# A spectral filter and MLP block, forward and backward: the fourth row block of h kept on chip, the other h loads put into spent slots, and all five engine orders laid out anew

## The chip, the core and the metric

The kernel runs on one core of a Trainium2 chip. The metric is the device time of one execution in microseconds (us); less is better. The times of the kernel before are 394.0, 394.21 and 395.75 us, median 394.21.

## The reference

An adaLN block on x of 2048 rows by 512, bf16, and its gradient. Six modulation rows come from a vector c; a spectral filter stands in the place of attention, an MLP with a squared ReLU behind it:

```python
mod = (silu(c) @ w_mod).reshape(c.shape[0], 6, 1, -1)
sa, ca, ga, sb, cb, gb = ...
h = layernorm(x) * (1 + ca) + sa
x = x + ga * irfft2(rfft2(h) * (w_r + 1j * w_i))
n = layernorm(x) * (1 + cb) + sb
h = relu(n @ w1 + b1) ** 2          # 2048 x 1792
x = x + gb * (h @ w2 + b2)
```

The outputs are the block's result and the gradients with respect to x, w_r, w_i, w1, b1, w2, b2, c and w_mod, ten in all. The gradient of w2 is h transposed times the scaled incoming gradient, the gradient of w1 is the normalized rows transposed times the gradient at h.

## The kernel before

Rows are worked on in 16 tiles of 128 (t), grouped in four blocks of 512 rows (b, NB = 4). The MLP's width of 1792 is cut into 14 chunks of 128 (fc, NFC = 14). The two-dimensional Fourier transforms are matmuls with constant matrices.

The stages, in the order in which the work is written:

- The start: filler matmuls on a tile of ones (L751, 30 of them), the modulation rows, the layernorm statistics (L819, L820), the constants TA of the transform (L119 to L130, on VectorE, ScalarE and TensorE), sacol (L757), the product L787 of sacol with a part of w_mod and its doubling gb2x (L789), w2 transposed and scaled by it (L796, L799), the first transform.
- back_products (L887): w2 transposed times the incoming gradient, written to gaT, a part of the large tile gall.
- The forward spectral pass.
- For each row block b: stage_g, stage_m and stage_t make the second layernorm and its transposes; stage_h (L1051) makes h and its gradient, seven pairs of chunks, each in a tile "h" of a ring of seven buffers, and writes each pair to h_dram (L1074); ghn_part (L1045) transposes the gradient at h from SBUF to SBUF into ghn, other rows of gall, 28 DMAs in all (gab<-gab in the trace); stage_gn and stage_o make the back product of the MLP and the block's result (L1096).
- The second spectral pass, backward (L1360 to L1425): its element-wise steps run on VectorE (L444 to L447, in cmul) and read Z and Xb from DRAM (L1373, L1377).
- grad_w1 (L1338 to L1349): 16 units that use ghn and h_sb, the normalized rows loaded back from DRAM at L1234. The first eight units, with fb 0 and 1, use the first seven chunks of ghn.
- The last row pairs (row_pair, L1504 on): VectorE and ScalarE finish the gradient of x, with gs, gh1 and q1 as ring tiles; colsums1 (L1499) sums gh1 and q1 on TensorE.
- grad_w2 (L1433 to L1443): 14 chunks of 16 matmuls of 128 by 512 in g_sb times hn, and g_sb is the gradient scaled by one modulation row (L1463). hn is a chunk of h with rows on the partitions, which the DMA transposes as it loads it from h_dram (load_hn, L1252 to L1257): 16 tiles of 128 by 128, 512 KB. The first two chunks lie in a pool hnp, the next two in a pool of the second pass, and the rest in a ring of six in the pool endp. After chunk fc, loads are issued up to the larger of fc + 4 and the smaller of 2 fc + 6 and 10.
- The modulation gradients (GMod: wmc loads L481, gm_junk on VectorE L500, gwm stores L502), and the tail.

Nearly all transfers are issued from SyncE (SP), whose queue is in order: an issue that waits holds back all issues behind it. The order of every engine's instructions is fixed by the table ORDER (L505 to L600): for each of the five engines it lists the instructions' numbers, by program position, in the order in which they are to run, and set_order (L603) ties each to the one before it.

```python
def set_order(tc):
    ...
    for name, runs in ORDER.items():
        todo = mine[ENGINES[name]]
        ...
        for before, after in zip(seq, seq[1:]):
            tc.add_manual_dep(after, before.name, edge, reason="order")
```

Of the kernel before, what the change touches and what calls it, by code (L numbers as in the profile page):

```python
# [18 lines left out]
D = 512  # L19
# [5 lines left out]
NB = 4  # L25
# [444 lines left out]
class GMod:  # L470
# [12 lines left out]
    def emit(self, jc, q, row, pool, ppool, nbuf=2, last=False):  # L483
# [1134 lines left out]
```

## Time and profile before

| what | value |
|---|---|
| times of the runs | 394.0, 394.21, 395.75 us |
| median | 394.21 us |
| the profiled execution's own time, from its first to its last instruction | 398.0 us |
| TensorE (PE) busy | 382.1 us, 96% |
| VectorE (DVE) busy | 334.8 us, 84% |
| ScalarE (ACT) busy | 303.2 us, 76% |
| HBM traffic | 181 GB/s over the span |
| mean granted TensorE clock | 0.990 |

The profile is one execution, and the trace gives 398.0 us for it, 3.8 us above the median of the timed runs. In the page each engine has a row of 40 slices, a digit for the busy share in tenths, and PEclk is the clock that TensorE was granted. The view of the waits has rows "engine output line <- what it waited for: us in total, times, longest". The chain of waits and the timelines give the start in us, then the duration in us. "SPq" is SyncE's queue: the time of such a row is that of the issue, and "to landing" is the time from issue until the data are there. L is the line in the kernel.

### The profile page before, as it was taken

Reading aid. Unit: us, or ns where it says so; the run is one execution under the profiler, and the core shown is the slowest. Engines: PE = TensorE matmul, PEld = TensorE weight load, DVE = VectorE, ACT = ScalarE, POOL = GpSimd, SP = SyncE. Lnnn points to the kernel's source line nnn. Section 1 sums busy time; section 2 is a strip of 40 time slices with the busy share of each in tenths; the row PEclk is TensorE's granted clock in tenths of the full one; section 3 lists DMA queues with packets and bytes.
Section 4 is the critical chain, followed back from the end, with each engine's and each line's share of the span. In section 5 each row is a group of like instructions: output and inputs, shape, how many; then the busy total and the mean of one; then the engine's idle time right before and its main releaser. Section 6 shows DMA issues by size and latency. Waiting matters only on the chain.

```text
span 398.0 us, 8415 instructions
## 1 busy us (share of the span) xinstructions
PE 382.1 (96%) x3042; PEld 202.4 (51%) x3042; DVE 334.8 (84%) x822; ACT 303.2 (76%) x605; POOL 33.3 (8%) x114
## 2 busy tenths in 40 slices
PE   8999999999999999999999999999999999999495
PEld 3555677544444444444444435457666664444244
DVE  8899959949986699969997999957999989998430
ACT  4787899899896499759976999277665589998441
POOL 9151001000000000000000000012300000002100
PEclk9999999999999999999999999999999999999979
DMA  8999799874589999578928696999979998999995
GB/s 258 362 222 293 230 209 252 209 280 63 195 228 197 256 259 253 128 191 183 257 81 210 167 245 180 270 245 371 296 221 262 215 325 173 221 208 243 249 259 189
DMA packets 133957, 91.06 MB, mean 229 GB/s; under 512 B 86842, under 2 KB 119868, under 8 KB 133660
## 3 DMA queue, kind: packets, MB, share of 16 engines
q1 hardware_dynamic: 132904, 88.09, 87.1%
q0 software_dynamic: 832, 2.36, 1.8%
q8 instruction: 24, 0.39, 0.4%
q14 instruction: 17, 0.14, 0.1%
q10 hardware_dynamic: 180, 0.07, 0.1%
HBM read 38.70 MB, written 33.19 MB: 181 GB/s over the span
## 4 chain that ended last, share of the span: by engine, by line
PE 74%; ACT 12%; DMA 5%; DVE 4%; POOL 2%; issue 1%; SPq 0%; ACTq 0%; POOLq 0%; DVEq 0%
PE og_1s L1096 12%; PE og_0s L1096 11%; PE mm_0s L1441 6%; PE mm_1s L1441 6%; PE mm_0s L1342 5%; PE mm_1s L1342 5%; PE mm_1s L1064 4%; PE mm_0s L1064 4%; PE pst L1064 3%; DMA hn_1s<-h_dram 3%; PE mm_0s L892 2%; DMA Xb<-xs_dram 2%; ACT AE L359 2%; PE mm_1s L892 2%; ACT gab L896 2%; ACT gab L1073 1%
## 5 line engine op out<-in xcount | busy, mean ns | idle before, releaser
L1342 PEld LDWEIGHTS <-h_sb 128*64 128x64 bf16 (+1 forms) x464 | 28.7, 109 | 15.9 <-issue 0.9
L1073 ACT ACTIVATE gab<-gab 128x512 bf16<-128x512 bf16 x56 | 35.0, 648 | 0.5 <-DVE gab L1071 0.5
L1096 PEld LDWEIGHTS <-gab 128*128 128x128 bf16 x224 | 21.5, 98 | 27.0 <-ACT gab L1073 1.9
L1064 PEld LDWEIGHTS <-w 128*128 128x128 bf16 x224 | 21.2, 98 | 25.7 <-issue 1.7
L1342 PE MATMUL mm_0s<-gab,h_sb 128*64 128x384 bf16 (+2 forms) x288 | 32.7, 345 | 0.0
L892 PEld LDWEIGHTS <-w2T 128*128 128x128 bf16 (+1 forms) x280 | 22.9, 102 | 18.5 <-issue 3.9
L1096 PE MATMUL og_0s<-w1T,gab 128*128 128x512 bf16 x112 | 27.4, 379 | 0.2 <-ACT G_0s L1109 0.2
L1096 PE MATMUL og_1s<-w1T,gab 128*128 128x512 bf16 x112 | 27.6, 379 | 0.0
L1441 PE MATMUL mm_0s<-g_sb,hn_1s 128*128 128x512 bf16 x64 | 16.8, 423 | 6.0 <-DMA hn_1s<-h_dram 6.0
L1342 PE MATMUL mm_1s<-gab,h_sb 128*64 128x512 bf16 (+2 forms) x176 | 22.4, 370 | 0.0
L1064 PE MATMUL mm_1s<-h2T,w 128*128 128x512 bf16 x84 | 21.9, 379 | 0.0
L1064 PE MATMUL mm_0s<-h2T,w 128*128 128x512 bf16 x80 | 21.2, 379 | 0.0
L359 ACT ACTIVATE AE<-psB 128x1024 bf16<-128x1024 f32 x16 | 17.2, 1078 | 0.7 <-PE psB L355 0.6
L896 ACT CAST gab<-mm_1s 128x512 bf16<-128x512 f32 x24 | 14.8, 615 | 2.3 <-PE mm_1s L892 2.2
L892 PE MATMUL mm_0s<-gT_0s,w2T 128*64 128x512 bf16 (+1 forms) x76 | 16.1, 380 | 0.2 <-DVE gab L894 0.2
L892 PE MATMUL mm_1s<-gT_0s,w2T 128*128 128x512 bf16 (+1 forms) x72 | 15.6, 379 | 0.1
L1064 PE MATMUL pst<-h2T,w 128*128 128x512 bf16 x60 | 15.6, 379 | 0.0
L892 PE MATMUL mm_1s<-gT_1s,w2T 128*128 128x512 bf16 (+1 forms) x68 | 14.9, 379 | 0.3 <-ACT gab L896 0.2
L892 PE MATMUL mm_0s<-gT_1s,w2T 128*128 128x512 bf16 (+1 forms) x64 | 15.1, 379 | 0.0
L1441 PEld LDWEIGHTS <-hn_1s 128*128 128x128 bf16 x64 | 6.8, 107 | 15.3 <-DMA hn_1s<-h_dram 6.2
L321 POOL MEMSET AE<- 128x4 bf16 x4 | 0.4, 110 | 162.4 <-PE mm_1s L1064 162.4
L1441 PE MATMUL mm_1s<-g_sb,hn_0s 128*128 128x512 bf16 (+1 forms) x64 | 13.7, 352 | 0.0
(650 smaller groups left out, 1064.3 us busy)
## 6 DMA issues: line engine op xcount, KB each, us to landing
w<-in_B_w_dram SPq DMA_DIRECT2D x2, 1792.0 KB, 10.4
Xb<-xs_dram SPq DMA_DIRECT2D x4, 514.0 KB, 7.9
Z<-wz_dram SPq DMA_DIRECT2D x4, 514.0 KB, 7.5
x_sb<-in_A_x_dram SPq DMA_DIRECT2D x4, 512.0 KB, 6.2
n_dram<-x_sb SPq DMA_DIRECT2D x4, 512.0 KB, 6.2
h_dram<-h2r SPq DMA_DIRECT2D x8, 256.0 KB, 2.4
h_sb<-h_dram SPq DMA_DIRECT2D x4, 512.0 KB, 5.4
g_sb<-in_grad_out_dram SPq DMA_DIRECT2D x2, 1024.0 KB
```

Source lines behind the costliest of these rows:

```text
L321: nc.gpsimd.memset(ae[:, :, :, 256:257], 0.0)
L359: nc.scalar.activation(dst, ps.rearrange("p r b (e f) -> p (r b) f e", e=2), AF.Copy, scale=EF_S)
L892: nc.tensor.matmul(ps[m], lhsT=w2T[:, dc, fc * P + m.start:fc * P + m.stop], rhs=gT[b][:, :, dc, :], start=(dc == 0), stop=(dc == 3), **pos)
L896: nc.scalar.copy(out=gaT[b][:, fc, :], in_=ps)
L1064: nc.tensor.matmul(ps, lhsT=w1[:, dc, (fc + i) * P:(fc + i + 1) * P], rhs=h2T[b][:, :, dc, :], start=(dc == 0), stop=(dc == 3))
L1073: nc.scalar.activation(gh[:, i, :], gh[:, i, :], AF.Copy, accum_out=gb1[:, b, fc + i:fc + i + 1])
L1096: nc.tensor.matmul(ps, lhsT=lhs(fc), rhs=rhs[:, fc, :], start=(fc == 0), stop=(fc == NFC - 1))
L1342: nc.tensor.matmul(blocks(ps[m], fb), lhsT=h2_sb[:, t, dc * P + m.start:dc * P + m.stop], rhs=gh_rows(t, fb), start=(t == 0), stop=(t == N ...
L1441: nc.tensor.matmul(ps[:, 0:w], lhsT=hns[fc][:, t, :], rhs=g_sb[:, t, c:c + w], start=(t == 0), stop=(t == NT - 1))
```

## The change

Its parts:

- h_dram holds three row blocks instead of four. stage_h writes the chunks of blocks 0 to 2 as before; for block 3 nothing is written, and hpair keeps the seven tiles of the ring.
- Those seven tiles are transposed by the DMA from SBUF to SBUF into a new tile hr, among stage_gn of block 3 ("turns"). h_rows returns rows of hr for the last four row tiles and rows of hn for the others.
- load_hn loads 12 row tiles instead of 16, 384 KB instead of 512, into slots of gall which held ghn for the first eight units of grad_w1: eight slots, chunk fc and chunk fc + 8 share one. After chunk fc, loads are issued up to chunk fc + 9. Four loads instead of two are issued at each of the two places in the program ahead of grad_w2.
- The rings of gs, gh1, q1 and gw in the last stages lie in other spent rows of gall (Ring and place, over "spare") instead of the pool endp. The pools hnp and endp are gone; gall is released at the end.
- A pool "early" takes n2rows of the even blocks, h2r, h2T and r, and is released ahead of stage_gn of block 3.
- The table ORDER is laid out anew on all five engines.

```diff
-    h_dram = dram.tile([NFC, P, NT * P], BF16, name="h_dram")
+    h_dram = dram.tile([NFC, P, (NT - TB) * P], BF16, name="h_dram")
...
+    early = Slots(tc, name="early", bufs=1)
...
-                    n2b[b] = rows.tile([P, TB, D], BF16, name="n2rows")
+                    n2b[b] = (rows if b % 2 else early).tile([P, TB, D], BF16, name="n2rows", bufs=1)
...
-                nc.sync.dma_start(h_dram[fc:fc + 2, :, sl].rearrange("a p s -> p a s"), h2)
+                if b < NB - 1:
+                    nc.sync.dma_start(h_dram[fc:fc + 2, :, sl].rearrange("a p s -> p a s"), h2)
+                else:
+                    hpair[fc] = h2
...
-                merge(stage_gn(b, UT), [x for p in zip(again, parts + [lambda: None]) for x in p])
+                hrp = Slots(tc, name="hrp", bufs=1, side="right")
+                hr = hrp.tile([P, NFC, TB, P], BF16, name="hr")
+                turns = [lambda fc=fc: nc.sync.dma_start(hr[:, fc:fc + 2].rearrange("p a j c -> p (a j) c"), hpair[fc].rearrange("p a s -> p (a s)"), transpose=True)
+                         for fc in range(0, NFC, 2)]
+                merge(stage_gn(b, UT), [x for p in zip(again, parts + [lambda: None], turns + [lambda: None]) for x in p])
...
+    spare = [NFC * b + 6 for b in range(NB)] + [NFC * b + k for b in range(NB) for k in range(7, NFC)] + [NB * NFC, NB * NFC + 1]
+
+    def place(n):
+        a = next(a for a in spare if all(a + k in spare for k in range(n)))
+        for k in range(n):
+            spare.remove(a + k)
+        return gall[:, a:a + n, :]
+
+    class Ring:
+        def __init__(self, n, k):
+            self.tiles, self.k = [place(n) for _ in range(k)], 0
+
+        def tile(self):
+            self.k += 1
+            return self.tiles[(self.k - 1) % len(self.tiles)]
...
-            pool = hnp if fc < 2 else endp.get("hn", endp["gw"])
-            hns.append(pool.tile([P, NT, P], BF16, name="hn", bufs=2 if pool is not endp.get("hn") else 6))
+            a = NFC * (fc % 4) + 3 * (fc // 4 % 2)
+            hns.append(gall[:, a:a + 3, :].rearrange("p a (j c) -> p (a j) c", c=P))
             nc.sync.dma_start(hns[fc], h_dram[fc, :, :], transpose=True)
+
+    def h_rows(fc, t):
+        return hns[fc][:, t, :] if t < NT - TB else hr[:, fc, t - (NT - TB), :]
...
-                nc.tensor.matmul(ps[:, 0:w], lhsT=hns[fc][:, t, :], rhs=g_sb[:, t, c:c + w], start=(t == 0), stop=(t == NT - 1))
+                nc.tensor.matmul(ps[:, 0:w], lhsT=h_rows(fc, t), rhs=g_sb[:, t, c:c + w], start=(t == 0), stop=(t == NT - 1))
...
-        while len(hns) < min(NFC, max(fc + 4, min(2 * fc + 6, 10))):
+        while len(hns) < min(NFC, fc + 9):
             load_hn()
...
-                    endp["hn"] = endp["gm"] = Slots(tc, name="endp", bufs=2)
+                    endp["gs"], endp["gh1"], endp["q1"], endp["gw8"] = Ring(2, 6), Ring(2, 3), Ring(2, 3), Ring(1, 8)
...
     "PE": (
-        "0-7 30 8-13 31 14-16 52-59 17-22 32-47 23-26 64-67 27 60-63 28 76-83 29 68-75 89-93 237-240 84-88 99-103 241-242 245-246 "
+        "1 0 3 2 4 6 8 5 10 7 9 30 11-13 15 14 17 19 52 31 16 53-54 18 55 32-47 56-59 20-21 23 64-67 60-63 25 27 29 76-83 68-75 "
```

In the changed kernel the lines stand lower: the h write is L1084, ghn_part L1058, the hr transposes L1244, the h_sb loads L1251, load_hn L1288, grad_w1 L1376 to L1383, the scaling of g_sb L1497, grad_w2 L1475 and L1477; at the start the fillers are L758, sacol L764, gb2x L796, the statistics L826.

First place, SyncE at the end of the program, before. hn_0s to hn_3s are chunks of h, wmc the parts of w_mod for its gradient, out_6 the gradient of w2, gxl rows for the gradient of x.

```order
L481 DMA wmc_0s_5631<-in_w_mod_dram 128x4x512
L1443 DMA out_6_dram<-gw_1s_5350 128x512
L1257 DMA_TRANSPOSE hn_0s_5723<-h_dram_65 128x16x128
L1334 DMA gxl_1s_5519<-gx1_dram_62 128x1024
L1257 DMA_TRANSPOSE hn_1s_5774<-h_dram_65 128x16x128
L1443 DMA out_6_dram<-gw_2s_5374 128x512
L1257 DMA_TRANSPOSE hn_2s_5796<-h_dram_65 128x16x128
L481 DMA wmc_1s_5633<-in_w_mod_dram 128x4x512
L1257 DMA_TRANSPOSE hn_3s_5824<-h_dram_65 128x16x128
L1443 DMA out_6_dram<-gw_3s_5450 128x512
```

And now, where gab is gall and holds the chunks of h as well as the tiles of gw:

```order
L1477 DMA out_6_dram<-gab_145 128x512
L1436 DMA out_2_dram<-Xb_4067 32x4x257
L1477 DMA out_6_dram<-gab_145 128x512
L1433 DMA out_2_dram<-Xb_4067 32x2x1028
L1288 DMA_TRANSPOSE gab_145<-h_dram_65 128x12x128
L1368 DMA gxl_5344<-gx1_dram_62 128x1024
L1368 DMA gxl_1s_5502<-gx1_dram_62 128x1024
L481 DMA wmc_0s_5611<-in_w_mod_dram 128x4x512
L1477 DMA out_6_dram<-gab_145 128x512
L481 DMA wmc_1s_5613<-in_w_mod_dram 128x4x512
```

The row with h_dram is the last of the 14 loads. Before, four loads stand among the last stores and the wmc loads; now the last one stands ahead of both wmc loads, and the others stand further up.

Second place, SyncE around block 3's last stages, before. h_2s to h_6s are the pairs of h, gab<-gab the transposes of the gradient at h, LFb and Cdb constants of the second pass, h_sb the rows for grad_w1.

```order
L1074 DMA h_dram<-h_4s 128x2x512
L1228 DMA LFb_3510<-LF_dram 128x1024
L1228 DMA LFb_3509<-LF_dram 128x1024
L1049 DMA_TRANSPOSE gab<-gab 128x8x128
L1074 DMA h_dram<-h_6s 128x2x512
L1074 DMA h_dram<-h_5s 128x2x512
L1049 DMA_TRANSPOSE gab<-gab 128x8x128 x2
L1134 DMA gx_dram<-n2rows_1s 128x1024
L1234 DMA h_sb<-h_dram 128x2048 x2
```

And now:

```order
L1244 DMA_TRANSPOSE hr<-h_3s 128x8x128
L1244 DMA_TRANSPOSE hr<-h_0s 128x8x128
L1058 DMA_TRANSPOSE gab<-gab 128x8x128
L1244 DMA_TRANSPOSE hr<-h_2s 128x8x128
L1146 DMA gx_dram<-n2rows 128x1024
L1251 DMA h_sb<-h_dram 128x2048
L1244 DMA_TRANSPOSE hr<-h_6s 128x8x128
L1244 DMA_TRANSPOSE hr<-h_4s 128x8x128
L1058 DMA_TRANSPOSE gab<-gab 128x8x128
L1236 DMA Cdb<-Cd_dram 128x512
L1251 DMA h_sb<-h_dram 128x2048 x3
```

Where plain writes of h stood, transposes of h into hr stand, three ahead of the first h_sb load and two more ahead of the last three.

Third place, VectorE at the start, before. ta_v is what TA is made from, l_st and l_mv are the layernorm statistics of x, gen_v and lf the parts of other constants.

```order
L119 SCALAR_TENSOR_TENSOR ta_v<-kh,pidf,kh_off 128x128
L755 CAST ccolf<-sm_ps 128x4
L121 TENSOR_SCALAR ta_v<-ta_v 128x128
L757 TENSOR_TENSOR sacol<-sigcol,ccolf 128x4
L176 TENSOR_SCALAR gen_v_1s<-cf_dr,cf_f_1180 128x128
L764 CAST scf<-sacol 128x4
L176 TENSOR_SCALAR gen_v_1s<-cf_dr,cf_f_1180 128x128
L819 BN_STATS l_st_0s<-x_sb 128x6
L819 BN_STATS l_st_2s<-x_sb 128x6
```

And now, from the first statistic on; sacol follows 12 rows further down, behind the next aggregate and parts of lf:

```order
L826 BN_STATS l_st_2s<-x_sb 128x6
L224 TENSOR_SCALAR lf_ph<-lf_tf 128x1 x2
L227 TENSOR_SCALAR lf_ph<-lf_tf 128x1
L826 BN_STATS l_st_3s<-x_sb 128x6
L826 BN_STATS l_st_0s<-x_sb 128x6
L227 TENSOR_SCALAR lf_ph<-lf_tf 128x1
L827 BN_AGGR l_mv_1s<-l_st_3s 128x2
L231 TENSOR_SCALAR lf_mk<-lf_sm,lf_tf 128x16
L119 SCALAR_TENSOR_TENSOR ta_v<-kh,pidf,kh_off 128x128
```

Three statistics stand ahead of ta_v and of sacol, where they stood behind both.

More of the change, by code (lines that the diff above doesn't have):

```diff
@@ L963 @@
         ghn = [None] * NB
+        hpair = {}
         late, late_f1 = Delayed(4), Delayed(4)
@@ L1015, in one @@
                 t = TB * b + j
-                h2r = rows.tile([P, 2, D], BF16, name="h2r", bufs=1)
+                h2r = early.tile([P, 2, D], BF16, name="h2r")
                 nc.vector.tensor_tensor(h2r, n2b[b][:, j:j + 2, :], modb[:, CB1_B, None, :].broadcast_to([P, 2, D]), op=ALU.mult)
@@ L1021, in one @@
                     if j == 0:
-                        h2T[b] = rows.tile([P, TB, 4, P], BF16, name="h2T", bufs=1)
+                        h2T[b] = early.tile([P, TB, 4, P], BF16, name="h2T")
                     K["h2T"] = nc.sync.dma_start(h2T[b][:, j:j + 2].rearrange("p j c q -> p (j c) q"), h2r.rearrange("p j d -> p (j d)"),
@@ L1030, in one @@
                 if j == 0:
-                    h2T[b] = rows.tile([P, TB, 4, P], BF16, name="h2T", bufs=1)
+                    h2T[b] = early.tile([P, TB, 4, P], BF16, name="h2T")
                 pst = psR.tile([P, D], FP32, name="pst2").bitcast(BF16).rearrange("p (c i q) -> p c i q", c=4, i=2)
@@ L1056, in stage_h @@
             for fc in range(0, NFC, 2):
-                r = rows.tile([P, 2, SB], BF16, name="r")
+                r = early.tile([P, 2, SB], BF16, name="r", bufs=2)
                 for i in range(2):
@@ L1219 @@
             else:
+                early.release()
                 w1p.release()
@@ L1248 @@
     gm = GMod(tc, K, scf, gsc, wm_view, out9_view)
-    hnp = Slots(tc, name="hnp", bufs=1, side="right")
     hns, endp = [], {}
+    spare = [NFC * b + 6 for b in range(NB)] + [NFC * b + k for b in range(NB) for k in range(7, NFC)] + [NB * NFC, NB * NFC + 1]
[10 more added lines that the diff above has]
+            return self.tiles[(self.k - 1) % len(self.tiles)]
     def load_hn():
@@ L1422, in after_b @@
                     K["g_load"] = nc.sync.dma_start(endp["g_sb"][:, t:t + 8, :], g_view[:, t:t + 8, :]).ins
-                load_hn()
-                load_hn()
+                for _ in range(4):
+                    load_hn()
         spec_f23(tc, K, UT, AEs, None, lambda gi: gwa.tile([P, 2, 2, FP], BF16, name="G", bufs=2), ew_b, after_b)
@@ L1434, in grad_w2 @@
         if cols[0] == 0:
-            late_ = "gm" in endp
-            gwh[fc] = (endp["gm"] if late_ else gwp).tile([P, D], BF16, name="gw", bufs=8 if late_ else 2)
+            late_ = "gw8" in endp
+            gwh[fc] = endp["gw8"].tile()[:, 0, :] if late_ else gwp.tile([P, D], BF16, name="gw", bufs=2)
         gw = gwh[fc]
@@ L1452, in grad_b2 @@
         add_quadrants(ps, gwp, out_7[None, :])
-    for _ in range(2):
+    for _ in range(4):
         load_hn()
@@ L1484, in fill @@
                     gwa.release()
-                    gap.release()
-                    endp["hn"] = endp["gm"] = Slots(tc, name="endp", bufs=2)
+                    endp["gs"], endp["gh1"], endp["q1"], endp["gw8"] = Ring(2, 6), Ring(2, 3), Ring(2, 3), Ring(1, 8)
                     endp["q"] = Slots(tc, name="endq", bufs=2)
@@ L1505, in row_pair @@
             n1, gxl = rows3[t]
-            gh1, q1 = [(endp["gm"].tile([P, 2, D], BF16, name=x, bufs=3) if "gm" in endp and t >= 6 else fp.tile([P, 2, D], BF16, name=x, bufs=2)) for x in ("gh1", "q1")]
+            gh1, q1 = [(endp[x].tile() if "gs" in endp and t >= 6 else fp.tile([P, 2, D], BF16, name=x, bufs=2)) for x in ("gh1", "q1")]
             gn = fp.tile([P, 2, D], BF16, name="gn")
-            gs = (endp["gm"].tile([P, 2, D], BF16, name="gs", bufs=6) if "gm" in endp and t >= 6 else fp.tile([P, 2, D], BF16, name="gs", bufs=3))
+            gs = (endp["gs"].tile() if "gs" in endp and t >= 6 else fp.tile([P, 2, D], BF16, name="gs", bufs=3))
             rr = fp.tile([P, 2, 4], FP32, name="rr")
@@ L1576 @@
     lf2.release()
-    hnp.release()
     h2p.release()
+    hrp.release()
     cdp.release()
@@ L1582 @@
     endp["q"].release()
-    endp["gm"].release()
+    gap.release()
     set_order(tc)
```

171 rows, old and new, of the table ORDER are left out of this document.

## The prediction

> **What bounds the kernel now.** I read the page first, for which engine fills the span and where it does not.
>
> ```profile
> span 398.0 us, 8415 instructions
> PE 382.1 (96%) x3042; PEld 202.4 (51%) x3042; DVE 334.8 (84%) x822; ACT 303.2 (76%) x605; POOL 33.3 (8%) x114
> PE   8999999999999999999999999999999999999495
> PEclk9999999999999999999999999999999999999979
> ```
>
> TensorE is busy for 96% of the span. The clock row and the PE row dip together once, near the end; every other slice after the first is full. So there are two sorts of gain: less PE work, of which the change removes none, or the dip. The view of the waits, for PE, says how large the dip is:
>
> ```profile
> PE mm_0s L1441 <- DMA hn_1s<-h_dram: 6.0, 1, 6.0
> PE mm_0s L751 <- DVE ones_sq L83: 1.8, 1, 1.8
> PE psB L355 <- ACT AE L359: 0.8, 2, 0.7
> PE psW_1s L796 <- ACT gT_0s L811: 0.4, 1, 0.4
> ```
>
> One wait of 6.0 us, for a transposed load of h; the 1.8 us are ahead of filler matmuls at the start; the rest is under a microsecond each. The chain of waits gives the same place in time, and SyncE's timeline shows the queue that fed it (start, duration of the issue):
>
> ```profile
> 366.24 12.07 DMA hn_1s<-h_dram
> 378.36 5.97 PE mm_0s L1441 x16
> 384.33 3.45 PE mm_1s L1441 x16
> ```
>
> ```profile
> 361.15 4.37 SPq L1257 DMA_TRANSPOSE hn_0s<-h_dram  x1
> 366.24 5.22 SPq L1257 DMA_TRANSPOSE hn_1s<-h_dram  x1
> 372.41 7.57 SPq L1257 DMA_TRANSPOSE hn_2s<-h_dram  x1
> DMA to landing us min/median/max: 4.9/5.7/12.1
> ```
>
> The load of chunk hn_1 was issued at 366.24, and PE was ready for it at 378.36 − 6.0 = 372.4, so it had 6.2 us; its median landing is 5.7 us (last row, L1257's), but this one took 12.1. Then the first unit of 16 matmuls after the gap takes 5.97 us where the next takes 3.45: the slow clock of the dip costs a further 2.5 us. The stall is thus worth 6.0 + 2.5 = 8.5 us.
>
> The view of stages shows what the transfers and VectorE have left (us, PE busy, PEld, DVE, ACT, POOL, then PE clock, DMA share, GB/s):
>
> ```profile
> 235.00:262.00 27.00, 26.78 (x165) 12.30 (x163) 26.29 (x59) 16.81 (x37) 1.31 (x5) 1.00 0.90 236
> 262.00:300.00 38.00, 37.09 (x500) 25.93 (x500) 30.84 (x75) 25.80 (x42) 6.76 (x15) 1.00 0.94 292
> 300.00:345.00 45.00, 45.00 (x512) 25.41 (x509) 42.97 (x97) 34.80 (x72) 0.00 (x0) 1.00 0.96 241
> 345.00:372.00 27.00, 27.00 (x150) 12.41 (x149) 24.24 (x58) 24.48 (x49) 4.54 (x9) 1.00 1.08 223
> 372.00:384.00 12.00, 6.04 (x20) 2.24 (x19) 2.02 (x6) 4.14 (x8) 0.33 (x1) 0.72 1.15 247
> ```
>
> The DMA engines are full from 235 on, and past full from 345; PE's clock is 1.00 until 372. So the transfers are the second bound, and VectorE (43.0 of 45 us between 300 and 345) is the third.
>
> **The loads of h (the gain).** Each of the 14 loads shrinks from 16 to 12 rows, 512 to 384 KB, and goes into a slot that grad_w1 has finished with, up to nine chunks ahead. Chunk 13 has the slot of chunk 5, so its load can start when unit 5 is done, with units 6 to 12 still ahead of its own; in the order (the first place shown) it now stands ahead of both wmc loads and the last stores of gw, where before it came behind both. A unit is 3.45 us, so a lead of up to 7 × 3.45 = 24 us replaces 6.2, where even the worst landing was 12.1. Per microsecond of PE work the loads of the last third also ask for a quarter less. I take the whole stall as gone: −6.0 and −2.5. What is late next: the wmc loads stood in front of the last hn loads before and now follow them, but only the modulation gradient's tail needs them, beside about 24 us of PE units.
>
> **Block 3's h, on chip.** Seven writes of 256 KB go; seven DMA transposes of 256 KB SBUF to SBUF come. The near row is the kernel's own transposes of gab, the same shape (issue, then landing), against the landing of the h writes (L1074):
>
> ```profile
> L1049 SPq DMA_TRANSPOSE gab<-gab x28: 1231/1239/2031, 128.2 to 262.2; - x28
> DMA to landing us min/median/max: 3.1/3.1/5.4
> SPq L1049 <- DMA gab<-gab: 19.9, 17, 3.3
> DMA to landing us min/median/max: 2.2/2.9/8.7
> ```
>
> Low end 7 × 1.24 = 8.7 us of the queue, if only the issue counts; high end 7 × 3.1 = 21.7, if nothing overlaps. The writes that go carried 256 KB each; at the stage's 236 GB/s for a share of 0.90 (262 GB/s if full) that is 1.0 us each, 7.0 together. The queue gets 1.7 to 14.7 us more to do. Free in it are 0.10 × 27 = 2.7 and 0.06 × 38 = 2.3, so 5.0 us up to 300: loads behind come 0 to 9.7 us late. The page "DMA: Bandwidth & Descriptors" of the Trainium skill, section "Latency and other measured facts", gives DMA transposes an effective 261 GB/s; by it seven would take an estimated 7.0 us, no more than the writes, and nothing would be late; the row's 3.1 us each stays above that here.
>
> Who waits for those loads:
>
> ```profile
> L1234 SPq DMA_DIRECT2D h_sb<-h_dram x4: 339/512/596, 246.0 to 248.8; - x4
> DMA to landing us min/median/max: 5.1/5.4/5.7
> 259.18 0.62 PE L1342 MATMUL mm_0s<-gab,h_sb 128*64 128x512 bf16 x4
> 270.37 0.70 DVE L444 TENSOR_TENSOR p<-Z,G_0s 128x1028 bf16<-128x1028 bf16 x1 [4.22 <-ACT G_0s L339]
> 274.58 0.70 DVE L445 TENSOR_TENSOR p<-Xb,G_0s 128x1028 bf16<-128x1028 bf16 x1 [0.88 <-DMA Xb<-xs_dram]
> ```
>
> The h_sb loads have 259.18 − 248.8 = 10.4 us, of which landing takes 5.1 to 5.7, so about 5 us of slack. VectorE waits 4.2 us for ScalarE at 270 and 0.9 for Xb at 274.58: here a late Xb moves VectorE at once. What VectorE loses reaches PE only at the end of the row pairs:
>
> ```profile
> 363.11 0.68 DVE L1517 TENSOR_TENSOR q_1s<-gh_1s,n_1s 128x1024 bf16<-128x1024 bf16 x1
> 366.07 0.38 PE L1499 MATMUL acc<-q_1s,ones_q 128*32 128x512 bf16 x1
> ```
>
> which is 2.9 us of slack. In the middle of the bounds (4.9 late) some 2 us would show at PE, and none of it if PE units can be set before it; since the order was laid out anew with grad_w2 units around, I take 0 here, and keep 0 to 6.8 for the range.
>
> **The start.** VectorE's first rows are in another order (the third place shown): three statistics of x now stand ahead of the TA constants and of sacol, from which the first PE product follows.
>
> ```profile
> 6.13 0.15 DVE L757 TENSOR_TENSOR sacol<-sigcol,ccolf 128x4 bf16<-128x4 f32 x1
> 6.66 0.69 DVE L819 BATCH_NORM_STATS2 l_st_0s<-x_sb 128x6 f32<-128x512 bf16 x1
> 10.94 0.16 DVE L789 TENSOR_SCALAR gb2x<-sm_ps 128x4 f32<-128x4 f32 x1 [0.33 <-PE sm_ps L787]
> 14.69 1.02 PE L892 MATMUL mm_0s<-gT_0s,w2T 128*128 128x512 bf16 x4
> ```
>
> Three at about 0.6 us apart are 1.8 us, and VectorE may stand before the first until x has landed, at the latest 6.66. sacol then comes at 8.7 to 10.4 instead of 6.13; the product and gb2x, 10.94 now, need it plus 0.5 us plus a statistic and a lf_v that have come between (about 1.1): 10.9 to 12.5, so 0 to +1.6. From 14.69 on PE is dense, and what is lost there stays: I take +0.8.
>
> **The rest.** The new rings in gall, the early pool, the constant of two and the table loads change addresses, not work; shape switches of PE are 62 before and 59 now, by the order, with no row that prices them: 0, and at most the waits under a microsecond listed above, 0.8 + 0.4 + 0.2: ±1.6. The g_sb load stands on SyncE behind a load or store that waits for the last gm_junk of VectorE's second pass; VectorE's first use of g_sb now stands 9 rows after that gm_junk, 14 before:
>
> ```profile
> 310.44 0.74 DVE L500 SCALAR_TENSOR_TENSOR gm_junk<-wmc_1s,onef,gmbc 128x512 bf16<-128x512 bf16 x1
> 319.06 2.36 DVE L1463 TENSOR_TENSOR g_sb<-g_sb,modb 128x2048 bf16<-128x2048 bf16 x2 [0.68 <-DMA g_sb<-in_grad_out_dram]
> ```
>
> 14 rows in 8.6 us are 0.6 a row; five rows less are 3.1 us less lead, and it already waits 0.7. Less the 2.9 us of slack that is 0 to 0.2, taken as 0.
>
> **The sum.** 398.0 − 6.0 − 2.5 + 0.8 = 390.3 for the profiled execution. That execution is 398.0, the median of the runs 394.21: 3.8 above. If the 3.8 lie in the stall, the one place of that size, the median's stall is only 4.7, and the result is 394.2 − 4.7 + 0.8 = 390.3. If they are spread evenly (398.0/394.21 = 1.0096), 390.3 becomes 386.6. The clock row, 1.00 until the stall, speaks for the first; I go a little toward the second: **389.5**.
>
> **The rivals.**
>
> *The transposes block the queue (slower).* Place: SyncE between 225 and 262, where five of the seven hr transposes stand ahead of the last three h_sb loads (the second place shown) and all ahead of Z and Xb. Each waits for its own h, and transposes on this queue wait for one another (19.9 us in 17 waits, 1.2 each). At 3.1 + 1.2 each, seven cost 30.1; less 7.0 and 5.0, loads come up to 18 late, PE 18 − 2.9 = 15 late. It decides from the point at which 2.9 + 7.7 = 10.6 us of lateness eat the gain; at 13 late, PE loses 10.1 and the result is about 399.6. For it: VectorE already waits for Xb. Against it: seven are only a quarter of 28 such transposes that cost PE nothing in the trace.
>
> *The wait moves (no change).* The h_sb loads have 5 us of slack and five transposes now ahead of the last three; 5 × (1.24 to 3.1) is 6.2 to 15.5 us. In the lower half PE waits about 4 us at 259, or for an early hn: 389.5 + 4 = 393.5. For it: the queue is in order. Against it: the loads are also asked for from rows further up.
>
> *The change doesn't do what it says (no change).* Transposed bytes are the same in all, 14 × 512 = 7168 KB before and 14 × 384 + 7 × 256 = 7168 now, and the queue's share was 1.08 to 1.15 where the stall stood. If bytes and not order set the arrival, a wait of some 3 us stays, with its slow clock: 389.5 + 3.0 + 1.3 = 393.8. Against it: a quarter of them has moved before 262.
>
> *The slow clock returns at the start.* In the new order the transposition of TA stands behind 18 of the 30 filler matmuls of L751 (14 before) and waits for ta_v, now behind the statistics: by the delay of sacol above, 2.6 to 4.3, less the four fillers, PE idles for about 2 to 3 us before it. If the clock then drops as it did after the 6.0 us wait, the next work costs 2.5 us more: 392.0. The page "TensorE: Matmul & The Clock Gate" of the Trainium skill, section "What's actually happening", says that an idle window of about 3.4 us halves the clock and as long a busy one restores it; the 6.0 us wait and the 5.97 for 3.45 agree, and by that rule an idle of 2 us would leave the clock up.
>
> **How the numbers follow.** Forecast 0.55; blocked queue 0.17; moved wait 0.12; bytes, not order 0.10; start clock 0.06. A measurement of this kernel tells about 0.5% (2.0 us) from no change: faster is below 392.2, slower above 396.2. The start clock's case falls on the faster side: 0.55 + 0.06 = 0.61, a little less for the forecast's own upper end: 0.60. The two middle cases give 0.22; the blocked queue, with the upper ends of the moved wait, 0.18. The range goes down to the even stretch without a start cost and without small waits (386.6 − 0.8 − 0.8 = 385.0), and up into the blocked queue, 398.0, so that about half of that case and a little below are left out.
>
> **What would show it.** Right: PE's view of the waits has no row on h_dram above 1 us, the clock row stays at 9 to the end, SyncE's last hn issue lies over 15 us ahead of its unit. The start: PE's first w2T product at 14.7 to 16.3. Wrong: a new row of several microseconds at the first grad_w1 unit (h_sb), at p on Z or Xb with PE waiting for q or G later, or a clock dip before 20 us.

## The result and the profile after

| | before | after |
|---|---|---|
| times of four runs each on one chip, us | 394.0, 394.21, 394.44, 395.75 | 402.82, 403.16, 403.57, 403.95 |
| median, us | 394.32 | 403.37 |
| profiled execution: span, us | 398.0 | 401.8 |
| its mean granted clock | 0.990 | 1.000 |

The changed kernel is slower: 1.0225 times before, interval 1.0202 to 1.0248. The prediction was 389.5 (385 to 398), faster. The time of after's profiled execution is 403.57, its span 401.8. In the experiments below a ratio leaves out executions that lie over 1.5% above the fastest of their kernel, while a median keeps them, so the two can differ.

The page of after answers to the first lines shown of before: PE's busy time, its row in 40 slices, and the clock row.

```profile
span 401.8 us, 8407 instructions
PE 383.4 (95%) x3042; PEld 204.9 (51%) x3042; DVE 337.2 (84%) x822; ACT 305.1 (76%) x605; POOL 36.0 (9%) x114
PE   8999997979999999999999989999699999999996
PEclk9999999999999999999999999999999999999999
```

The dip near the end is gone from both rows, as forecast. In its place PE's row has a 7 in slices 7 and 9 (60 to 90 us) and a 6 in slice 29, with the clock at full. So the new loss is time in which PE stands idle. Two of these three slices lie early; the third, at 281 to 291, holds waits of 1.7, 0.5 and 1.1 us. To see when it arises, the same line of code is taken in both traces with its first and last start (the two times). Before, the last products of back_products, one matmul of the MLP's products, grad_w1 and the last unit of grad_w2:

```profile
L892 PE MATMUL mm_1s<-gT_1s,w2T x68: 376/379/403, 34.5 to 102.5; 128*128 128x512 bf16 x44, 128*64 128x512 bf16 x24
L1096 PE MATMUL og_1s<-w,h_6s x16: 379/379/379, 120.8 to 257.9; 128*128 128x512 bf16 x16
L1342 PE MATMUL mm_0s<-gab,h_sb x288: 326/326/403, 259.2 to 327.8; 128*64 128x384 bf16 x80, 128*64 128x512 bf16 x48, 128*128 128x384 bf16 x16
L1441 PE MATMUL mm_0s<-g_sb,hn_3s x32: 272/326/379, 358.6 to 392.8; 128*128 128x512 bf16 x16, 128*128 128x256 bf16 x16
```

And after:

```profile
L899 PE MATMUL mm_1s<-gT_1s,w2T x68: 376/379/403, 35.5 to 107.9; 128*128 128x512 bf16 x44, 128*64 128x512 bf16 x24
L1108 PE MATMUL og_1s<-w,h_6s x16: 379/379/379, 126.2 to 266.8; 128*128 128x512 bf16 x16
L1376 PE MATMUL mm_0s<-gab,h_sb x288: 325/326/403, 267.6 to 340.9; 128*64 128x384 bf16 x80, 128*64 128x512 bf16 x48, 128*128 128x384 bf16 x16
L1475 PE MATMUL mm_0s<-g_sb,hr x32: 272/379/379, 350.8 to 398.3; 128*128 128x512 bf16 x24, 128*128 128x256 bf16 x8
```

PE is 1.0 late at 34.5, 5.4 at 102.5, 8.9 at 257.9, 13.1 at 327.8 and 5.5 at the end, after the stall that before's execution had. About two thirds of the lateness thus arise ahead of 258 us, and 4.2 us behind it. Where the first 5 us come from is in the view of PE's waits, cut to 15 to 108 us (in total, times, longest). Before:

```profile
PE mm_1s L892 <- ACT gab L896: 0.2, 1, 0.2
PE psT L401 <- ACT Tsb_0s L403: 0.2, 1, 0.2
PE mm_0s L892 <- DVE gab L894: 0.2, 1, 0.2
```

After:

```profile
PE psC_1s L338 <- POOL AE L361: 2.1, 1, 2.1
PE psG_1s L385 <- DVE utcs L389: 0.8, 1, 0.8
PE psG_0s L385 <- DVE utcs L389: 0.8, 1, 0.8
PE mm_0s L899 <- ACT gab L903: 0.8, 2, 0.6
PE psT L401 <- ACT Tsb_0s L403: 0.6, 2, 0.3
PE mm_1s L899 <- ACT gab L903: 0.5, 1, 0.5
```

Before sums to 0.6, after to 5.6: nothing large, and no edited buffer among them. Five of after's eight waits, 4.3 us, are the transform's own steps (psC, psG, psT) waiting for one another; the other three are back_products waiting for ScalarE's copies. PE's timeline of after gives the places (start, duration, count, and in brackets the wait):

```profile
66.07 0.41 PE L338 MATMUL psC_1s<-AE,LF 128*64 128x257 bf16 x4 [2.13 <-POOL AE L361]
...
81.24 0.41 PE L385 MATMUL psG_0s<-LG,Z 64*128 64x128 bf16 x12 [0.78 <-DVE utcs L389]
...
85.40 0.41 PE L385 MATMUL psG_1s<-LG,Z 64*128 64x128 bf16 x12 [0.79 <-DVE utcs L389]
```

And VectorE's, ahead of the second of them:

```profile
80.49 0.69 DVE L389 CAST utcs<-psG_0s 128x512 bf16<-128x512 f32 x1 [0.60 <-PE psG_0s L385]
```

VectorE waits 0.60 for PE's psG, then PE 0.78 for VectorE's copy of it: the two take turns, and in after's order no w2T matmul stands between these two steps of PE. In before the same steps, between 72 and 81 us, pass without a wait of PE. The 2.13 are a step of POOL that takes 2.69 us where it took 0.60 at most before; the last section returns to it.

### The profile page after: what moved, and what is told of

Its sections match the earlier page's. It is cut to its first block, busy times and chain, and to the rows that moved or that the text cites. A ratio compares the mean times of both kernels' runs of the same rounds, so it can differ in the third digit from the quotient of the medians.

```text
span 401.8 us, 8407 instructions
## 1 busy us (share of the span) xinstructions
PE 383.4 (95%) x3042; PEld 204.9 (51%) x3042; DVE 337.2 (84%) x822; ACT 305.1 (76%) x605; POOL 36.0 (9%) x114
## 4 chain that ended last, share of the span: by engine, by line
PE 64%; DVE 14%; ACT 8%; DMA 6%; SPq 4%; issue 2%; POOL 1%; ACTq 0%; DVEq 0%; POOLq 0%
PE og_1s L1108 6%; PE og_0s L1108 6%; PE mm_1s L1475 6%; PE mm_0s L1475 6%; PE mm_1s L1376 5%; PE mm_0s L899 4%; PE mm_1s L899 4%; PE mm_0s L1376 4%; PE mm_1s L1073 3%; PE mm_0s L1073 3%; PE pst L1073 2%; SPq L1244 2%; DMA Z<-wz_dram 1%; PE mod_ps L779 1%; ACT gab L903 1%
## 5 line engine op out<-in xcount | busy, mean ns | idle before, releaser
L1376 PEld LDWEIGHTS <-h_sb 128*64 128x64 bf16 (+1 forms) x464 | 30.7, 109 | 14.4 <-issue 0.5
L1108 PEld LDWEIGHTS <-gab 128*128 128x128 bf16 x224 | 21.7, 98 | 26.5 <-ACT gab L1082 1.4
L1376 PE MATMUL mm_0s<-gab,h_sb 128*64 128x384 bf16 (+2 forms) x288 | 33.7, 344 | 0.0
L899 PEld LDWEIGHTS <-w2T 128*128 128x128 bf16 (+1 forms) x280 | 23.9, 102 | 17.9 <-issue 2.6
L1475 PEld LDWEIGHTS <-gab 128*128 128x128 bf16 x192 | 18.5, 98 | 17.2 <-issue 0.9
L1376 PE MATMUL mm_1s<-gab,h_sb 128*64 128x512 bf16 (+2 forms) x176 | 23.7, 370 | 0.0
L1073 PE MATMUL mm_1s<-h2T,w 128*128 128x512 bf16 x84 | 22.9, 379 | 0.5 <-ACT r_1s L1074 0.5
L1475 PE MATMUL mm_1s<-g_sb,gab 128*128 128x512 bf16 (+1 forms) x96 | 20.5, 352 | 0.0
L1475 PE MATMUL mm_0s<-g_sb,gab 128*128 128x512 bf16 (+1 forms) x96 | 19.5, 352 | 0.0
L1073 PE MATMUL pst<-h2T,w 128*128 128x512 bf16 x60 | 17.3, 379 | 0.0
L899 PE MATMUL mm_0s<-gT_1s,w2T 128*128 128x512 bf16 (+1 forms) x64 | 16.3, 379 | 0.3 <-ACT gab L903 0.2
```

Source lines behind the costliest of these rows:

```text
L899: nc.tensor.matmul(ps[m], lhsT=w2T[:, dc, fc * P + m.start:fc * P + m.stop], rhs=gT[b][:, :, dc, :], start=(dc == 0), stop=(dc == 3), **pos)
L1073: nc.tensor.matmul(ps, lhsT=w1[:, dc, (fc + i) * P:(fc + i + 1) * P], rhs=h2T[b][:, :, dc, :], start=(dc == 0), stop=(dc == 3))
L1108: nc.tensor.matmul(ps, lhsT=lhs(fc), rhs=rhs[:, fc, :], start=(fc == 0), stop=(fc == NFC - 1))
L1376: nc.tensor.matmul(blocks(ps[m], fb), lhsT=h2_sb[:, t, dc * P + m.start:dc * P + m.stop], rhs=gh_rows(t, fb), start=(t == 0), stop=(t == N ...
L1475: nc.tensor.matmul(ps[:, 0:w], lhsT=h_rows(fc, t), rhs=g_sb[:, t, c:c + w], start=(t == 0), stop=(t == NT - 1))
```

## The experiments

The expectations name theories by letters: A is the new order of the engines, B the transposes of hr in SyncE's queue; the others are told in the texts. Where an experiment splices two orders, "the first T as before" means: the instructions that before's trace starts ahead of T us come first, in before's order, on each engine; the rest follows in after's order. The seven writes of h and the seven transposes into hr stand for each other. The diff then gives how many entries at the head of each row of ORDER are before's. Behind a median stand its lowest and highest run in brackets. Ratios are to the kernel before on the same chip, with the interval in brackets; differences in us are between medians, most of them from different chips, and so the rougher measure.

**The first 220 us as before.** The program of after, all its buffers and loads:

```diff
 ORDER, entries at the head of each row taken from before's
-PE 0, ACT 3, DVE 0, POOL 0, SP 1
+PE 1555, ACT 307, DVE 480, POOL 79, SP 141
```

> The changed kernel, but with what ran in the first 220 us of the kernel before put back into the order that it had there, on all five engines; the rest of the new order follows. In the trace of the changed kernel TensorE reached its first grad_w1 matmul 8.4 us later than before (267.6 against 259.2), 7 of them by 220 us. Theory A (the new order of the first 220 us costs the time): that comes back, 403.4 - 7 = 396 us. Theory B (the hr transposes hold SyncE's queue): nothing of the first 220 us touches it, 402 to 403 us. Theory C (the shared addresses of the early pool cost the time, whatever the order): 403 us.

Measured: 395.32 (394.22 to 396.41), ratio 1.0001 [0.9971, 1.0031]; 8.1 us less than after by medians, about 8.8 by the ratios (1.0225 against 1.0001, of 394.3). PE's lines in its trace, to be read against the two blocks above:

```profile
L899 PE MATMUL mm_1s<-gT_1s,w2T x68: 376/379/403, 34.3 to 102.3; 128*128 128x512 bf16 x44, 128*64 128x512 bf16 x24
L1108 PE MATMUL og_1s<-w,h_6s x16: 379/379/379, 120.5 to 259.2; 128*128 128x512 bf16 x16
L1376 PE MATMUL mm_0s<-gab,h_sb x288: 325/326/403, 260.0 to 331.4; 128*64 128x384 bf16 x80, 128*64 128x512 bf16 x48, 128*128 128x384 bf16 x16
L1475 PE MATMUL mm_0s<-g_sb,hr x31: 272/379/379, 341.8 to 389.3; 128*128 128x512 bf16 x23, 128*128 128x256 bf16 x8
```

At 102.3 it stands where before stood (102.5), and at the end it is 9.0 ahead of after (389.3 against 398.3). The order of the first 220 us, and neither the buffers nor the loads, makes after slower than before. With it put back, the rest of the change just pays for itself.

**Before, with its first 80 us in after's order.** The same splice the other way:

```diff
 ORDER of before, entries at the head of each row taken from after's
-PE 0, ACT 3, DVE 0, POOL 0, SP 1
+PE 713, ACT 107, DVE 228, POOL 79, SP 57
```

> The kernel before, but with what ran in the first 80 us of the changed kernel put into the changed kernel's order, on all five engines; the rest as before. Nothing of the loads of h, of gall or of the pools is changed. Theory A: the new order alone costs 4 to 5 us here, 394.3 + 4.5 = 398.8 us, less what the wait for hn near the end takes in. Theories B and C: no change, 394.3 us.

Measured: 409.11 (406.49 to 413.69), ratio 1.0332 [1.0251, 1.0413]. As a time this tells little, because the seam made a wait of its own, which neither kernel has. The profiled execution is also the slowest of the four, and its wait for hn_1s, a row of the kernel before, has grown to 9.5 us. Beside it:

```profile
PE mm_0s L892 <- ACT gab L896: 6.5, 2, 5.9
PE psC_1s L338 <- POOL AE L361: 2.1, 1, 2.1
```

The second row is the one of after, 2.1 us, now in before's program: order alone makes it. By 82 us, ahead of the seam's wait, PE was 3.9 late.

**Without the transposes of hr.** The last four row tiles of grad_w2 use the rows of the first four instead, so that part of its result is another:

```diff
-                turns = [lambda fc=fc: nc.sync.dma_start(hr[:, fc:fc + 2].rearrange("p a j c -> p (a j) c"), hpair[fc].rearrange("p a s -> p (a s)"), transpose=True)
-                         for fc in range(0, NFC, 2)]
+                turns = [lambda: None] * 7
...
-        return hns[fc][:, t, :] if t < NT - TB else hr[:, fc, t - (NT - TB), :]
+        return hns[fc][:, t % (NT - TB), :]
```

> The changed kernel without the seven hr transposes: they are left out, and the last four row tiles of grad_w2 use the rows of the first four. Same matmuls, same other transfers, same order. Theory B: Z comes at about its place of before against the work around it, and TensorE gets back the 4.5 us that it lost between 262 and 330, and more if the transposes also slowed what was ahead: 399 us or below. Theory A: the order costs the same as before, 403 us; at most 1 us back.

Measured: 403.81 (402.99 to 404.86), ratio 1.0222 [1.0166, 1.0278]: nothing gained. Yet the transposes do what the first rival said. SyncE's timeline of after has them ahead of Z:

```profile
264.93 3.72 SPq L1244 DMA_TRANSPOSE hr<-h_5s  x1
268.69 1.31 SPq L1244 DMA_TRANSPOSE hr<-h_1s  x1
...
277.14 0.61 SPq L1407 DMA_DIRECT2D Z<-wz_dram  x1
```

In before the same issue of Z starts at 263.79, 13.3 us earlier, and VectorE's first product p waits 6.0 us for it in after, by its view of waits. Without hr, grad_w1's last matmul starts at 336.0 instead of 340.9. The 4.9 us are lost again near 380, in the view of PE's waits and in ScalarE's timeline of the kernel without hr:

```profile
PE mm_1s L1474 <- ACT gab L1475: 2.1, 2, 1.6
```

```profile
373.74 0.72 ACT L1548 ACTIVATE gab<-gn_0s,inv 128x512 bf16<-128x512 bf16 x1 [4.58 <-DVE gn_0s L1546]
...
381.48 0.56 ACT L1475 CAST gab<-mm_1s 128x512 bf16<-128x512 f32 x1
```

The copy of a finished unit of grad_w2 stands in ScalarE's queue behind the row pairs' gn and gab, which wait for VectorE; PE then waits for the copy. Behind the wait of 1.6 the clock falls, and a unit takes 3.35 us instead of 1.91 (the last section has the rows). By these rows the row pairs set the end there, and PE coming earlier helps nothing; no run changed the row pairs to confirm it. Theory B falls for the time, not for the mechanism.

**Before, with its last four loads of hn further up.** Only SyncE's row of ORDER changes; hn loads go ahead of gxl, wmc and two stores of gw:

```diff
 SyncE of before, around its last four loads of hn (other rows left out)
-gxl  gxl_0s  wmc_0s  gw store  hn  gxl_1s  hn  gw store  hn  wmc_1s  hn  gw store
+hn  gxl  hn  gxl_0s  gxl_1s  hn  wmc_0s  gw store  hn  gw store  wmc_1s  gw store
```

> The kernel before, with only SyncE's order changed near the end: the last four loads of hn stand ahead of the gxl and wmc loads and the stores of gw by which they stood behind. Sizes and slots as before. The stall theory of the prediction: the wait for hn and the slow clock behind it go, 8.5 us of the profiled execution and about 4.7 of the median: 389.6 us (386 to 390). Rival (the bytes set when hn lands, not the order): 393 to 394.3 us, with a wait of some microseconds left.

Measured: 402.5 (400.98 to 403.72), ratio 1.0185 [1.0126, 1.0245]. No wait for hn is left, but the stores that were passed now come late, and the copy that needs their ring slot:

```profile
PE mm_1s L1441 <- ACT gw_2s L1442: 8.8, 1, 8.8
PE mm_0s L1441 <- ACT gw_1s L1442: 1.5, 1, 1.5
```

**The same, with the stores kept in place.**

```diff
-hn  gxl  hn  gxl_0s  gxl_1s  hn  wmc_0s  gw store  hn  gw store  wmc_1s  gw store
+hn  gw store  gxl  gxl_0s  hn  gxl_1s  gw store  hn  wmc_0s  hn  wmc_1s  gw store
```

> The kernel before, SyncE's order changed near the end as in the earlier run with early hn loads, but with the stores of gw kept ahead of the loads that follow them, since there ScalarE waited 11.4 us for such a store. Theory: the stall for hn is small in most executions of before (mean clock 0.99 in the profiled one, 0.996 to 1.0 in most), so taking it away gives 0 to 3 us: 392 to 394.5 us. Prediction's size: 389.6 us. If the stores of gw wait again: 397 us or more, with ScalarE's gw copy waiting for a store in the trace.

Measured: 398.13 (395.76 to 399.73), ratio 1.0033 [0.9987, 1.0079]: no gain. The wait is still there with another name, for the store of gw_3 behind the last hn load:

```profile
PE mm_0s L1441 <- ACT gw_3s L1442: 5.7, 1, 5.7
```

```profile
375.11 3.52 SPq L1257
379.31 4.57 DMA out_dram<-gw_3s
384.59 3.57 PE mm_0s L1441 x16
```

In both of these orders the wait for a load of hn becomes a wait for a store of gw: the queue as a whole is late at 375 in before's ring of buffers. That agrees with what the third rival said of the kernel before, as far as two orders can show it; after, which has no such wait, has more slots and smaller loads as well as another order.

**The first 220 us as before and no hr.** The two edits of the first and third experiment together.

```diff
 ORDER, entries at the head of each row taken from before's
-PE 0, ACT 3, DVE 0, POOL 0, SP 1
+PE 1555, ACT 307, DVE 480, POOL 79, SP 141
...
+                turns = [lambda: None] * 7
```

> The first 220 us in the order of before, and the hr transposes left out too (the last four row tiles of grad_w2 use the rows of the first four). With the first 220 us put back alone the kernel took 395.3 us. Leaving hr out alone, the middle of the trace (300 to 340) came 5 us earlier, but the end did not. Theory B2 (the transposes cost the second half 4 us, and the end follows when nothing else is late): 391 us. Theory D (the row pairs and the stores at the end set the time whenever the middle comes earlier): 394 to 395.5 us.

Measured: 396.58 (394.87 to 399.27), ratio 1.0011 [0.9965, 1.0057]. hr is no cost at the end here either: PE waits 1.9 and 0.8 us for ScalarE's copies, and the clock falls behind the longer one, as above.

**The first 105 us as before.**

```diff
 ORDER, entries at the head of each row taken from before's
-PE 0, ACT 3, DVE 0, POOL 0, SP 1
+PE 994, ACT 159, DVE 284, POOL 79, SP 67
```

> The changed kernel with only the first 105 us put back into the order of before. Theory A, summed from the trace (TensorE 5.4 us late at the end of that stretch): 403.4 - 5.4 = 398 us. If what is lost early is absorbed later: 401 to 403 us.

Measured: 396.51 (395.71 to 398.14), ratio 1.0016 [0.9979, 1.0053]: 6.9 us less than after, more than the 5.4 that the lateness of PE at that point promised. Nearly all of the loss comes from the first quarter of the program. What after's own order from 105 to 220 adds is about 1 us (395.32 against 396.51), which the intervals of the two ratios don't separate; in the traces the first grad_w1 matmul starts 1.3 us later (261.3 against 260.0).

**The first 220 us as before on all engines but SyncE.**

```diff
 ORDER, entries at the head of each row taken from before's
-PE 0, ACT 3, DVE 0, POOL 0, SP 1
+PE 1555, ACT 307, DVE 480, POOL 79, SP 1
```

> As the run with the first 220 us in the order of before, but SyncE keeps the changed kernel's order; TensorE, VectorE, ScalarE and GpSimd have that of before. Theory A1 (what stands behind what on the computing engines, and what covers a wait on TensorE, costs the time): 395 to 397 us. Theory A2 (the transfers' order costs it): 402 to 404 us.

Measured: 399.04 (396.92 to 400.45), ratio 1.0079 [1.0045, 1.0113]: 4.3 us less than after, between the two expectations. By 105 us its PE has made up 5.2 of the 5.4, so the early loss is the computing engines' order. Later SyncE's order, laid out for the other one, brings a load late, and PE waits 1.9 us for the weights of a row block (og on w). The two belong together.

**Before's order outside 220 to 262 us, on the program of after.** SyncE from 220 on in after's order; then SyncE in before's as well:

```diff
 ORDER, entries of before's at the head, and at the tail of each row
-PE 0 and 64, ACT 3 and 3, DVE 0 and 9, POOL 0 and 0, SP 1 and 1
+PE 1555 and 1245, ACT 307 and 158, DVE 480 and 203, POOL 79 and 24, SP 141 and 1
```

> The changed kernel's program, with the order of before for all that ran there in the first 220 us (five engines) and for all that ran after 262 us on TensorE, VectorE, ScalarE and GpSimd; only the stretch about row block 3's last stages, and SyncE from 220 us on, keep the new order. Theory A (the new order of the second pass costs the 4 us that TensorE still lost between 262 and 330 with the first 220 us put back): 395.3 - 4 = 391 us, or a ratio of 0.990 to the kernel before on the same chip. Theory D (what is gained in the middle is lost at the end to another wait): ratio 1.000.

```diff
-SP 141 and 1
+SP 141 and 9 (and before's order between, but for 220 to 262)
```

> As the run with the order of before outside 220 to 262 us, with SyncE too in that order after 262 us: the last loads of hn stand behind the wmc loads and the stores of gw again, but are 384 KB instead of 512 and have eight slots. If the place of the loads in SyncE's order makes the stall: it is back, mean clock 0.99 to 0.996, ratio 1.000 to 1.005. If their bytes make it: clock 1.0, the same time as with the new order of SyncE, ratio 0.990.

Measured: 406.25 (404.25 to 407.95), ratio 1.0274 [1.0205, 1.0343], and 406.26 (400.19 to 407.8), ratio 1.018 [1.0078, 1.0282]. Both are slower than the kernel with only the first 220 us as before, so before's order gains nothing in the second half, against theory A. How far before's order there is itself to blame stays open: both kernels are spliced at 220 and 262 us, and have waits of a size that neither original has there, 2.9 and 3.0 us in the first one and the 4.0 below in the second. The second kernel has the wait for h back, though its load carries 384 KB as in after:

```profile
PE psB L355 <- ACT AE L359: 4.8, 2, 4.0
PE mm_0s L1475 <- DMA gab<-h_dram: 2.9, 1, 2.9
```

So the smaller loads alone left half of the 6.0 us standing; it went only with their earlier place.

**Where in the first 105 us.** Three cuts, the last one with after's own first 60 us and before's order from there to 220:

```diff
 ORDER, entries at the head of each row taken from before's
-PE 0, ACT 3, DVE 0, POOL 0, SP 1
+first 60: PE 495, ACT 79, DVE 198, POOL 79, SP 51
+first 15: PE 87, ACT 23, DVE 76, POOL 60, SP 13
+60 to 220: behind after's own first PE 468, ACT 77, DVE 191, POOL 110, SP 43
```

> The changed kernel with only the first 60 us in the order of before. Theory A, from the trace: TensorE was 2.0 us late there, 3.4 more came between 60 and 105: ratio 1.0225 - 2/394 = 1.017. If the whole loss of the first 105 us is made at the start (sacol, the statistics): ratio 1.002 to 1.006.

> The changed kernel with only the first 15 us in the order of before: the TA constants, sacol and the product ahead of the statistics again. The prediction's term for the start was 0.8 us (0 to 1.6), and the trace of the changed kernel has the first w2T product 1.2 us late: ratio 1.0225 - 1.2/394 = 1.0195. If the start is worth more than it shows there, because all of the first pass follows from it: ratio 1.008 to 1.015.

> The changed kernel in its own order for the first 60 us, in the order of before from there to 220 us, and in its own after that. It is the complement of the run with the first 60 us put back (ratio 1.0079). If the losses of the two stretches add up to the 8 to 9 us of the whole first 220 us: 1.0225 + 1.0001 - 1.0079 = 1.015. If TensorE's cover between 60 and 105 is the greater part, as the trace of the changed kernel has it (3.4 us of 5.4, and 1.5 more by 220): ratio 1.010.

Measured: 398.44 (396.98 to 401.34), ratio 1.0079 [1.0048, 1.0111]; 401.44 (399.39 to 405.58), ratio 1.0114 [1.003, 1.0198]; 400.74 (399.05 to 403.68), ratio 1.0119 [1.0012, 1.0225]. By medians that is 4.9 less than after's 403.37 with the first 60 us put back, 1.9 with the first 15 and 2.6 with 60 to 220; 4.9 and 2.6 make 7.5 of the 8.1. By ratios it is 5.8, 4.4 and 4.2, and 5.8 and 4.2 make 10.0 of the 8.8. Either way the first 60 hold the larger part, although after's eight waits all end behind 60: with the first 60 as before the POOL wait of 2.1 at 66 us is gone too. The intervals of the kernels with 15 and with 60 to 220 put back are as wide as the effects, so the division is rough, and whether the first 15 cost 2 or 4 us stays open.

## Why the prediction was wrong

**The stall goes: right.** After has no wait of PE on h_dram and no dip of the clock. The last load is issued at 379.6 and the first unit of its chunk starts at 394.9, 15.3 us ahead where over 15 was named, and landing takes 5.2 to 5.8. The two experiments on before's loads did not gain the time by moving them alone, in the old ring.

**What the stall was worth: too much, by its own reckoning.** The prediction put before's profiled execution at 398.0 us, 3.8 above the median. But 398.0 is the span. In 64 runs of before the time exceeds the span by 1.8 to 2.2 us, so that execution took about 400.0, 5.8 above its median. The 5.8 had to be taken off 8.5 and left 2.7 for the median, not 4.7. Before's times go with the mean granted clock of the execution: at 0.999 to 1.000 ten runs gave 393.0 to 397.0, at 0.991 eight gave 395.8 to 400.4; the profiled one had 0.990. That the stall is what varies is a reading: the half clock behind the hn wait is the one place of that size in before's only trace, and the wait was 9.5 us at a mean clock of 0.979 in before with its first 80 us in after's order. The lowest run of all, 393.0, lies 1.3 under the median of 394.3 here, and 4.3 under the median of its own chip, 397.3. So the usual worth can't be said more closely than some 1 to 4 us, since no run removes the stall alone.

**"The rest … change addresses, not work: 0 … ±1.6": the step that failed.** The new orders were looked at where buffers had changed and at the start, and the rest was put at nothing. The order of the first 220 us costs 8.1, that of the first 105 alone 6.9 (8.8 and 8.2 by the ratios). No term, no rival and no bound held it. The loss needs no large wait: from 15 to 108 us it is 5.0 us more, in eight waits where before has three.

**The start: right in sign and size, by luck.** First w2T product at 15.87 in after, at 14.69 in before: +1.2 for a bound of 0 to 1.6 and 0.8 taken. sacol came at 9.54, inside the 8.7 to 10.4 that was named, but it delayed nothing: gb2x starts at 10.75 against 10.94. The lateness arises behind it, on a way that the prediction did not have: ScalarE's copy gT_0s starts 0.6 later (13.84 against 13.28), and four filler matmuls then stand ahead of the transposes of w2 that need it. PE's timeline of after:

```profile
9.40 0.23 PE L128 MATMUL sm_ps<-ident,TA 128*128 128x128 bf16 x1 [0.39 <-ACT TA L124]
14.08 1.68 PE L758 MATMUL mm_0s<-ones_sq 128*128 128x512 bf16 x4
15.87 0.59 PE L899 MATMUL mm_0s<-gT_0s,w2T 128*128 128x512 bf16 x2
```

The transposition of TA waited 0.4, not 2 to 3, and the clock stayed up: the fourth rival did not arise.

**hr and Z: the mechanism of the first rival, without its price.** Z came 13.3 us later than before in these traces (8.9 of it because everything was late), and grad_w1 some 4.9 later than without hr. Of this the end shows nothing, because by the traces the row pairs' chain through VectorE and ScalarE is as late. The forecast took 0 here, and 0 was measured, but for another reason: it counted on grad_w2 units to fill the gap, and PE did lose the time in grad_w1. That rival's point of decision is also off: 2.9 + 7.7 = 10.6 sets the lateness against the gain of the profiled execution; against the median's gain of 4.7, from which its 399.6 is reckoned, it would be 7.6.

**The sum in hindsight**: with the first 220 us in before's order the ratio is 1.0001, so what the end of the stall gains (1 to 4 us) is lost again in the second half of after; 8.1 to 8.8 for the order of the first 220 makes the rest. The second half's loss can be seen in that kernel's trace, where grad_w1 ends 3.6 late (331.4 against 327.8; 330.4 without hr, so hr makes 1.0 of it). Behind 215 us its PE waits 4.8 us in nine waits, where before has 1.0 besides the stall; the two largest are

```profile
PE og_1s L1108 <- ACT gab L1082: 1.3, 1, 1.3
PE psC_1s L338 <- POOL AE L361: 1.1, 1, 1.1
```

These are steps of the same sort as in the first half, so the term put at nothing was missing there too; that the order makes them is argued here and not shown. Also open is how the first 60 us divide between the engines.

## What to carry to other kernels

When an order is laid out anew over the whole program, cost the whole of it: for each pair of dependent steps, how much of PE's work stands between them before and now (a method that no run here tried out); eight waits, seven of them under a microsecond, made 5.6 us here by 108 us. Before a stall's price is taken from a profile, set its execution (the span plus what the timed runs exceed theirs by, and its clock) against the timed runs, since a profile can hold more of a stall than the median does. A load moved up an in-order queue makes late what it passes: here the passed stores cost 8.8 and 1.5 us in place of a load's 6.0.

## What was not expected of the hardware

POOL's small correction of AE (L361, 64x8) is the step that PE waited 2.13 us for at 66.07. POOL's timeline of before, around the same steps:

```profile
59.91 0.23 POOL L361 TENSOR_TENSOR AE<-AE,one 64x8 bf16<-64x8 bf16 x1 [2.14 <-ACT AE L359]
62.30 0.48 POOL L361 TENSOR_TENSOR AE<-AE,one 64x8 bf16<-64x8 bf16 x1 [2.16 <-ACT AE L359]
```

And of after:

```profile
61.30 0.68 POOL L361 TENSOR_TENSOR AE<-AE,one 64x8 bf16<-64x8 bf16 x1 [2.63 <-ACT AE L359]
63.33 2.85 POOL L361 TENSOR_TENSOR AE<-AE,one 64x8 bf16<-64x8 bf16 x2 [1.35 <-ACT AE L359]
```

The longest of its sixteen takes 2.69 us after and 0.60 before, and 2.69 again in before's program with after's first 80 us; PE's wait for it at this place is still there in the kernel with the first 15 us as before, and is gone with the first 60 as before or with 60 to 220 as before. So it depends on when the engines come to this place. In after VectorE ran two-input products and sums without a break from 62.4 to 65.9 beside it, and the long step ended at 66.0. The Trainium skill, page "SBUF — State Buffer", section "🔬 SBUF: two separate sides", says that VectorE and GpSimd hold a shared pair of ports by an exclusive lock, also against a VectorE operation with two inputs in SBUF; the long row agrees with that. Before's row at 62.30 does not fit as well: it took 0.48 us while VectorE ran such sums from 62.27 to 63.04. No run here took VectorE's work away, so the lock is not shown to be the cause.

The clock can fall after a short wait. Stages of the kernel without hr (us, PE busy, PEld, DVE, ACT, POOL, PE clock, DMA share, GB/s):

```profile
379.00:382.00 3.00, 1.04 (x14) 0.19 (x5) 2.63 (x6) 2.78 (x8) 0.26 (x1) 1.00 1.07 203
382.00:385.40 3.40, 3.31 (x17) 2.42 (x17) 1.84 (x5) 1.67 (x4) 1.87 (x4) 0.55 0.83 252
```

The longest wait in the first was 1.58 us; in the second the clock was 0.55, and 16 matmuls took 3.35 us where 16 of the same width took 1.91 later. The other kernel without hr repeats it: a wait of 1.86 us, then a clock of 0.51 and 3.38 us. The fourth rival's sentence, that by the rule of the Trainium skill's page "TensorE: Matmul & The Clock Gate" an idle of 2 us would leave the clock up, is thus no safe bound where PE is thinly used around the wait; the measurement decides.
